# An output projection in 11 matmuls a token tile in place of 12, in a kernel with a planned instruction order

## The chip, the cores and the metric

The kernel runs on one core of a Trainium2 chip. The metric is device time in microseconds (us) of one execution; several executions are timed and the median is given. The engines are TensorE (PE in the profile, its weight loads PEld), VectorE (DVE), ScalarE (ACT), GpSimd (POOL) and SyncE (SP), which here only issues transfers between DRAM and the on-chip memory.

## What is computed

One transformer block on 2048 tokens of 448 features, in float32: layer norm, 16-head attention with 28 features a head and a sliding window of 256 keys, an output projection with a residual, then a second layer norm and a gated feed-forward of width 1792 with a residual.

```python
def _A_ref(x, wqkv, wo):
    B, S, D = x.shape
    H = 16; Dh = D // H; W = 256
    qkv = (x @ wqkv).reshape(B, S, 3, H, Dh).transpose(2, 0, 3, 1, 4)
    q, k, v = qkv[0], qkv[1], qkv[2]
    scores = einsum("bhqd,bhkd->bhqk", q, k) * (Dh ** -0.5)
    mask = (idx[:, None] - idx[None, :] >= 0) & (idx[:, None] - idx[None, :] < W)
    p = softmax(where(mask, scores, -1e9))
    o = einsum("bhqk,bhkd->bhqd", p, v)
    return o.transpose(0, 2, 1, 3).reshape(B, S, D) @ wo

h = x + _A_ref(layernorm(x), wqkv, wo)
y = layernorm(h)
h2 = h + (gelu(y @ w_gate) * (y @ w_up)) @ w_down
```

## The kernel before

**Precision by halves.** Matmuls run on a rounded float32 type (F32R). To keep float32 accuracy, most operands are split into a high half (ACT rounds it, `to_hi`, line 343) and a low half (the remainder, `to_lo`, line 346, on DVE or POOL). A product then takes three matmuls: high x high, high x low, low x high.

**An order made by a planner.** The kernel does not issue instructions as its loops run. Every `op(engine, cost, latency, key, ...)` only enters a list; `Lists.run` then plays the list through a small model of the engines, the 8 PSUM banks, the transfer queue and the port that DVE and POOL share, and emits each engine's instructions in the order in which the model starts them, smallest key first among those that are ready. The constants at the top (LAG_T, LAG_V, EDGE, LN1, LN2, VKEY, MARGIN, LEAD, FETCH and so on) set those keys and some of the model's delays. Each engine runs its list strictly in order on the chip.

**Stages.** Tokens go in four chunks `c` of 512 (four tiles of 128 each). For a chunk: layer norm (`layer_norms`, `normalise`), projections to queries and keys (`project`, seven of them, line 609, each 11 matmuls of 128x512) and to values (`values`, line 564), then four head groups `g` of four heads. A block `B = 4c + g` does scores (657) with a running maximum on DVE (661), the maxima turned and added to the queries (`maxima`, 678 to 692), the scores again the other way round with the exponential on ACT (`probs`, 729 and 733), masks on POOL (`select`, 744), and the product with the values (`attend`, 763).

**Projections go through DRAM.** A projected tile is drained from PSUM into a store buffer (high half by ACT, low half by DVE, lines 612 to 614) and stored by `put` (618, 619) in the form (high, low, high) or its mirror; `loads` (639) brings it back with the features of four heads side by side. The store buffers are given by `pk_at`: a ring of two, and two further ones in `pp` for the projections numbered in PKX.

**Turning normalised tiles.** Features must stand on partitions. `normalise` does it in one of two ways: PE transposes through a PSUM bank (398), then ACT and DVE split it; or, for the tiles in TURNED and for the second layer norm, `turn`: DVE transposes 32x32 blocks (435), four stores to DRAM (439), two loads back (441, 443), then ACT and DVE split it. In the kernel before, tiles 8 to 15 of the first layer norm are turned through DRAM.

**Drain and output.** `drain` (785 to 796) takes a block's result: DVE transposes it (788) into `oblk`, takes the reciprocal of the softmax sums (789), POOL multiplies (786), DVE transposes back (791), ACT and POOL split it into `ohl`. The last block does POOL's part on DVE. In `oblk` each head has 32 places, 28 features and 4 unused ones. After every second block `output` (807) multiplies a pair of groups by the rows of `wo`: for each token tile 2 groups x 3 products of 128x448, so 12 matmuls a tile over both pairs `p`, and DVE adds the result to the residual (810). `wo_weights` (816 to 818) loads and splits the rows of `wo` through one buffer.

**Feed-forward.** From about 341 us PE runs the products of line 945 without a break; a few early ones (969) stand in the last part of attention.

Of the kernel before, what the change touches and what calls it, by code (L numbers as in the profile page):

```python
# [33 lines left out]

LAG_T = 6
LAG_P = 15
LAG_V = 10
EDGE = 8
WIN = 14
FFN = 1000  # L40
LEAD = 90
MARGIN = 0.8
START = 0.8
EARLY = 2
SWAP = -60
HOLDO = 1
AHEAD = 7
BEHIND = 5
LN1 = (0, -20, 70, 134)
LN2 = (166, 231)  # L50
VKEY = (-30, -22, 14, 24)
VHALF = 0
FETCH = 200
POOLED = (3,)
PKX = (2, 3)
PAIRED = 4
TURNED = (8, 9, 10, 11, 12, 13, 14, 15)
# [168 lines left out]
def block_kernel(ctx: ExitStack, tc, x, wqk_in, wv_in, wo_in, ffn_in, out):  # L226
# [10 lines left out]
    def f(ap):  # L237
        return ap.bitcast(F32)
# [12 lines left out]
    one_r = pool.tile([128, 128], F32R, name="one")  # L251
    last_hi = pool.tile([128, 128], F32R, name="lasthi")

    word = pool.tile([128, 88], F32, name="word")
    nhalf = pool.tile([128, 4], F32, name="nhalf")
    e8 = pool.tile([128, 8], F32, name="e8")
    bnst = [pool.tile([128, 6], F32, name=f"bnst{i}") for i in range(2)]
    bnmv = pool.tile([128, 4, 2], F32, name="bnmv")
    bnve = pool.tile([128, 3, 4], F32, name="bnve")
    mx = [pool.tile([128, 2, 4], F32, name=f"mx{i}") for i in range(2)]  # L260
    mhl = [pool.tile([128, 96], F32R, name=f"mhl{i}") for i in range(3)]
    rcp = [pool.tile([128, 16], F32, name=f"rcp{i}") for i in range(2)]
# [54 lines left out]
    def PK(a):  # L317
        return span("proj", 3584 + 512 * a, 512)
# [29 lines left out]
    def dma(key, size, fn, r=(), w=(), cost=0.44, after=()):  # L348
        return op("sp", cost, 0, key, fn, r, w, size=size, after=after)
# [229 lines left out]
           [WQKRAW(m % 2), WQK(m, 0)], [WQK(m, 1)], port=True)  # L579


    pks = [0]

    def pk_at():
        n = pks[0]
        pks[0] += 1
        if n in PKX:
            o = 1792 + 1024 * PKX.index(n)
            return [pp_m[:, o + 512 * i:o + 512 * i + 512].bitcast(F32R) for i in range(2)], \
                pp_m[:, o:o + 1024].rearrange("p (a t) -> p a t", a=2), [span("pp", o // 128 + 4 * i, 4) for i in range(2)]  # L590
        n = sum(k not in PKX for k in range(n)) % 2
        return [pk[:, 2 * n + i] for i in range(2)], f(pk[:, 2 * n:2 * n + 2]), [PK(2 * n + i) for i in range(2)]

    def project(c):
        for m in range(WT):
# [2 lines left out]
    def project_tile(c, m):  # L598
        g, s = divmod(m, 2)
        cc = 12 * (c % 2)  # L600
        hl, both, tok = pk_at()
        B = 4 * c + g
        b = Bank("proj")
        per = 1 if m == 6 else 2
        base = 16 * B - EDGE
        for a in range(NP):
            h, wb, xb = TERMS[a]
            key = -33 + 6 * m + a / 4 if B < 2 else base - WIN * (1 - (s * NP + a) / (per * NP))
            op("pe", mm(512) + 0.002, 0.403, key, lambda a=a, h=h, wb=wb, xb=xb: nc.tensor.matmul(  # L609
                bank[b.k], wqk[m][:, h, wb, :], xT[:, xb, cc * 128:cc * 128 + 512], start=(a == 0),  # L610
                stop=(a == NP - 1)), [span("xT", cc, 4), WQK(m, h)], (), b, tag="proj")
        key = -30 + 6 * m if B < 2 else base
        op("act", 0.49, 0.605, key, lambda: to_hi(hl[0], bank[b.k]), (), [tok[0]], b)
        op("dve", 0.603, 0.698, key, lambda: to_lo(hl[1], bank[b.k], hl[0]), [tok[0]], [tok[1]], b)


        def put(rows, d, name, s, size):
            dma(key, 458 * size, lambda: nc.sync.dma_start(d[:, s:s + 2], both[rows]), tok, [(name, 0)])
            dma(key, 229 * size, lambda: nc.sync.dma_start(d[:, 2 - 2 * s], both[rows, 0]), tok[0:1], [(name, 1)])
        put(slice(0, GF), qk_d[g][c][s], ("d", g, s, c), s, 1)  # L620
        put(slice(GF, 128), qk_d[NG - 1][c][1][16 * m:16 * m + 16], ("d", NG - 1, 1, c, m), 1, 0.15)

# [152 lines left out]
    def drain(B):  # L775
        b, h = acc[B], B % 2
        key = 16 * B + LAG_P + ORDER[5] + LAG_V + 1
        rc = rcp[h]
        ob = oblk.rearrange("p (b r) -> p b r", r=32)


        last = B == NB - 1
        eng, name = (nc.vector, "dve") if last else (nc.gpsimd, "pool")

        def mul():
            eng.tensor_tensor(ob, ob, rc[:, :, None].to_broadcast([128, 16, 32]), op=OP.mult)

        op("dve", 0.63, 0.72, key, lambda: nc.vector.transpose(oblk, bank[b.k]), (), ["oblk"], b)
        op("dve", 0.165, 0.26, key, lambda: nc.vector.reciprocal(rc, ob[:, :, DH]), ["oblk"], [("rcp", h)])
        op(name, 0.6 if last else 1.05, 0.7 if last else 1.06, key + 1, mul, ["oblk", ("rcp", h)], ["oblk"], port=True)  # L790
        op("dve", 0.625, 0.71, key + 2, lambda: nc.vector.transpose(oT, oblk), ["oblk"], ["oT"])
        op("act", 0.52, 0.63, key + 2, lambda: to_hi(ohl[:, h, 0], oT), ["oT"], [("ohl", h, 0)])
        if last:
            exps.append(L.ops[-1])
        op(name, 0.6 if last else 1.25, 0.7 if last else 1.29, key + 3, lambda: to_lo(ohl[:, h, 1], oT, ohl[:, h, 0], eng),
           ["oT", ("ohl", h, 0)], [("ohl", h, 1)], port=True)

    def output(p, c):
        B = 4 * c + 2 * p + 1
        key = 16 * B + LAG_P + ORDER[5] + LAG_V + 5  # L800
        for i in range(4):
            t = c * 4 + i
            k = Bank("task")
            wk = key + (i if B == NB - 1 else 3 * i)
            for a, (h, oh, wh) in enumerate((h, oh, wh) for h in range(2) for oh, wh in ((0, 0), (0, 1), (1, 0))):
                need = [("ohl", h, oh), ("wos", p, h, wh)] if a else [("ohl", h, 0) for h in range(2)] + [("wos", p, h, 0)]
                op("pe", mm(D), 0.38, wk, lambda a=a, h=h, oh=oh, wh=wh, i=i, k=k: nc.tensor.matmul(  # L807
                    bank[k.k][:, 0:D], ohl[:, h, oh, i * 128:(i + 1) * 128], wos[p][:, h, wh], start=(a == 0),
                    stop=(a == 5)), need, (), k, tag="task")
            op("dve", 0.533, 0.626, wk + 1, lambda t=t, k=k: nc.vector.tensor_tensor(  # L810
                hres[:, t, :], bank[k.k][:, 0:D], hres[:, t, :], op=OP.add), [HR(t)], [HR(t)], k)

    def wo_weights(g):
        p, h = divmod(g, 2)
        key = 20 + 16 * p + 5 * h
        dma(key - 20, 224, lambda: nc.sync.dma_start(wo_raw, wo_in[g]), (), [WORAW], after=[got[HOLDO]])
        op("act", 0.47, 0.57, key, lambda: to_hi(wos[p][:, h, 0], wo_raw), [WORAW], [("wos", p, h, 0)])
        op("pool", 1.1, 1.15, key, lambda: to_lo(wos[p][:, h, 1], wo_raw, wos[p][:, h, 0], nc.gpsimd),
           [WORAW, ("wos", p, h, 0)], [("wos", p, h, 1)], port=True)

# [127 lines left out]

    def seen(key, b):

        op("act", 0.08, 0.17, key, lambda: nc.scalar.activation(word[0:1, 0:1], bank[b.k][0:1, 0:1], AF.Copy), (),  # L951
           (), b)

    def product(n, i, c, k, gn, gi, down):
# [224 lines left out]
def layout(inputs):  # L1179

    import numpy as np

    def rows(w):

        w = np.concatenate([w, w[384:]])
        return w.reshape(4, 128, -1).transpose(1, 0, 2)

    wqkv = inputs["A_wqkv"]
    q = [wqkv[:, g * GF:(g + 1) * GF] for g in range(NG)]
    k = [wqkv[:, D + g * GF:D + (g + 1) * GF] for g in range(NG)]  # L1190
    own = [t for g in range(NG - 1) for t in (q[g], k[g])] + [q[NG - 1]]
    wo = np.zeros((NG, 4, 32, D), np.float32)
    wo[:, :, 0:DH] = inputs["A_wo"].reshape(NG, 4, DH, D)
    gate, up = inputs["B_w_gate"], inputs["B_w_up"]
    ffn = [np.concatenate([rows(gate[:, n:n + 128]).reshape(128, 512), rows(up[:, n:n + 128]).reshape(128, 512),
                           inputs["B_w_down"][n:n + 128]], axis=1) for n in range(0, F, 128)]
    return {"x": inputs["A_x"],
            "wqk": np.stack([rows(np.concatenate([t, k[NG - 1][:, 16 * m:16 * m + 16]], axis=1))
                             for m, t in enumerate(own)]),
            "wv": np.stack([rows(wqkv[:, 2 * D + 2 * GF * p:2 * D + 2 * GF * (p + 1)]) for p in range(2)]), "wo": wo.reshape(NG, 128, D), "ffn": np.stack(ffn)}  # L1200


# [19 lines left out]
```

## Time and profile before

| what | us |
|---|---|
| median of three runs | 733.01 (732.46 to 734.0) |
| the profiled execution, whole | 733.24 |
| its span, first to last instruction | 731.5 |

The page of the profile has the busy time of each engine, the span in 40 slices, the transfers, the chain of work that ended last, and groups of instructions by source line. "out<-in" names the tiles that an instruction writes and reads; a line such as L346 is that of a helper, so the tile names tell what it does. "Idle before" is the time for which an engine stood still just ahead of these instructions, with what it waited for. The granted clock of TensorE is full throughout. Matmul ends are modelled, so the time from one start to the next in a run of matmuls is a better price than the mean duration.

### The profile page before, as it was taken

How to read it: one execution, taken by the hardware profiler on the slowest of the kernel's cores; microseconds unless marked ns; L12 is line 12 of the kernel's file. 1: busy time of each engine (PE TensorE's matmuls, PEld its weight loads, DVE VectorE, ACT ScalarE, POOL GpSimd, SP SyncE). 2: the span in 40 equal slices, each digit the busy share in tenths (PEclk: the TensorE clock that was granted, in tenths of full speed). 3: DMA queues.
4: the chain of work that ended last, by engine and by line, in shares of the span. 5: the costliest groups of instructions: out<-in, count | busy, mean ns of one | idle time of the engine just before them, and what ended most of it. 6: DMA issues, size and time to landing. Idle time of an engine off the chain costs nothing.

```text
span 731.5 us, 15121 instructions
## 1 busy us (share of the span) xinstructions
PE 719.3 (98%) x5732; PEld 594.6 (81%) x5732; DVE 404.7 (55%) x1069; ACT 368.0 (50%) x934; POOL 155.7 (21%) x250
## 2 busy tenths in 40 slices
PE   8999999999999999999999999999999999999997
PEld 7886777777778787778888888888888888888886
DVE  7967778978798768858454223144223243233224
ACT  7647667787787678985443222243222233222221
POOL 5505443444344346541000000000000000000000
PEclk9999999999999999999999999999999999999999
DMA  8887787696677868341832000012100000001012
GB/s 307 268 269 234 207 251 184 179 260 200 176 184 196 224 190 239 86 111 26 199 120 84 1 1 3 1 42 84 43 1 1 2 1 1 2 1 51 7 46 101
DMA packets 102801, 83.80 MB, mean 115 GB/s; under 512 B 49272, under 2 KB 92472, under 8 KB 102712
## 3 DMA queue, kind: packets, MB, share of 16 engines
q1 hardware_dynamic: 102584, 82.72, 39.3%
q8 instruction: 45, 0.74, 0.4%
q14 instruction: 28, 0.23, 0.1%
q10 hardware_dynamic: 144, 0.11, 0.0%
HBM read 51.09 MB, written 31.95 MB: 114 GB/s over the span
## 4 chain that ended last, share of the span: by engine, by line
PE 91%; DMA 3%; ACT 3%; DVE 1%; issue 1%; SPq 0%; POOL 0%; DVEq 0%; ACTq 0%; POOLq 0%
PE bank L945 52%; PE bank L609 9%; PE bank L729 6%; PE bank L657 6%; PE bank L807 5%; PE bank L763 5%; PE bank L564 5%; PE bank L969 2%; DMA k<-proj 1%; ACT pp L733 1%; DMA xT<-xn 1%; DMA hres<-in_x_dram 1%; ACT xT L343 1%; ACT rq L343 0%; DMA xn<-xn 0%
## 5 line engine op out<-in xcount | busy, mean ns | idle before, releaser
L661 DVE CUSTOM_DVE_ANT_0 mt<-bank,mt 128x384 bf16<-128x384 f32 (+2 forms) x256 | 127.4, 525 | 33.0 <-PE bank L657 30.7
L733 ACT ACTIVATE pp<-bank 128x384 f32<-128x384 f32 (+2 forms) x352 | 123.0, 387 | 42.8 <-PE bank L729 37.4
L1011 DVE TENSOR_TENSOR mt<-bank,mt 128x512 f32<-128x512 f32 x54 | 37.1, 687 | 142.9 <-ACT mt L1009 142.9
L729 PE MATMUL bank<-rq,rk 104*128 104x384 f32 (+2 forms) x352 | 99.7, 306 | 3.1 <-ACT pp L733 1.7
L744 POOL TENSOR_SCALAR_AFFINE_SELECT pp<-pp 128x512 f32<-128x512 f32 x120 | 75.3, 641 | 110.3 <-ACT pp L733 108.7
L609 PE MATMUL bank<-xT 128*128 128x512 f32 x308 | 96.2, 401 | 0.0
L1009 ACT ACTIVATE mt<-bank 128x512 f32<-128x512 f32 x54 | 32.2, 596 | 118.3 <-PE bank L945 118.3
L729 PEld LDWEIGHTS bank<-rq,rk 104*128 104x128 f32 x352 | 65.3, 189 | 21.2 <-ACT pp L733 9.0
L945 PE MATMUL bank<-xT,rec 64*128 64x512 f32 x656 | 82.0, 388 | 0.0
L945 PE MATMUL bank<-xT,rk 64*128 64x512 f32 x656 | 82.0, 388 | 0.0
L657 PE MATMUL bank<-rk,rq 84*128 84x384 f32 (+2 forms) x256 | 80.3, 342 | 1.0 <-DMA rk<-k 0.8
L945 PEld LDWEIGHTS bank<-xT,rec 64*128 64x128 f32 x656 | 63.0, 184 | 12.2
L945 PEld LDWEIGHTS bank<-xT,rk 64*128 64x128 f32 x656 | 63.0, 184 | 12.2
L1047 DVE TENSOR_TENSOR hres<-bank,hres 128x448 f32<-128x448 f32 (+1 forms) x65 | 35.7, 610 | 66.5 <-PE bank L945 64.7
L945 PE MATMUL bank<-xT,proj 64*128 64x512 f32 x533 | 66.7, 388 | 0.3 <-ACT word L951 0.3
L951 ACT ACTIVATE word<-bank 1x1 f32<-1x1 f32 x162 | 25.6, 158 | 82.2 <-PE bank L945 81.6
L609 PEld LDWEIGHTS bank<-xT 128*128 128x128 f32 x308 | 55.7, 189 | 6.6 <-ACT xT L343 0.2
L945 PEld LDWEIGHTS bank<-xT,proj 64*128 64x128 f32 x533 | 51.1, 184 | 10.5 <-ACT word L951 0.6
L657 PEld LDWEIGHTS bank<-rk,rq 84*128 84x128 f32 x256 | 46.7, 189 | 11.7 <-issue 2.9
L564 PE MATMUL bank<-proj,xT 128*128 128x448 f32 (+1 forms) x220 | 51.1, 336 | 0.0
L343 ACT ACTIVATE rq<-bank 8x512 fp32r<-8x512 f32 x64 | 37.5, 586 | 17.6 <-PE bank L688 16.6
L763 PE MATMUL bank<-pp,v 128*29 128x384 f32 (+2 forms) x704 | 45.4, 388 | 0.0
(138 smaller groups left out, 1086.8 us busy)
## 6 DMA issues: line engine op xcount, KB each, us to landing
rk<-k SPq DMA_DIRECT2D x44, 336.0 KB
rq<-q SPq DMA_DIRECT2D x32, 336.0 KB
q<-proj SPq DMA_DIRECT2D x15, 448.0 KB
v<-in_ffn_dram SPq DMA_DIRECT2D x7, 736.0 KB
k<-proj SPq DMA_DIRECT2D x11, 448.0 KB
xn<-xn SPq DMA_DIRECT2D x88, 56.0 KB
xT<-xn SPq DMA_DIRECT2D x24, 192.0 KB
raw<-in_ffn_dram SPq DMA_DIRECT2D x6, 736.0 KB
```

Of the source, the lines that this page charges most:

```text
L343: nc.scalar.activation(dst, src, AF.Copy)
L564: op("pe", mm(224 * n), 0.29 if n == 1 else 0.38, key + a / 16, lambda a=a, h=h, wb=wb, xb=xb: nc.tensor.matmul(bank[b.k][:, 0:224 * n], x ...
L609: op("pe", mm(512) + 0.002, 0.403, key, lambda a=a, h=h, wb=wb, xb=xb: nc.tensor.matmul(bank[b.k], wqk[m][:, h, wb, :], xT[:, xb, cc * 128 ...
L657: nc.tensor.matmul(bank[b.k][:, o:384], rq[u][0:3 * DH, j, i * 128:i * 128 + 128], rk[u][0:3 * DH, j, m0 * 128:(i + 3) * 128], start=True, ...
L661: nc.vector.tensor_tensor_reduce(junk[s % 2][:, o:384], bank[b.k][:, o:384], mask[:, o:384], 1.0, -BIG, OP.add, OP.max, mx[i // 2][:, i % ...
L729: nc.tensor.matmul(bank[b.k][:, 0:n], rk[u][0:104, j, m * 128:m * 128 + 128], rq[u][0:104, j, lo * 128:(hi + 1) * 128], start=True, stop=True)
L733: nc.scalar.activation(pp[:, j, o * 128:o * 128 + n], bank[b.k][:, 0:n], AF.Exp, scale=SCALE)
L744: nc.gpsimd.affine_select(a, a, pattern=[[0, 4], [-cm, 128]], compare_op=op_, fill=0.0, base=0, channel_multiplier=cm)
L763: nc.tensor.matmul(bank[b.k][32 * j:32 * j + DH + 1, lo * 128:(hi + 1) * 128], v[:, at_v(4 * c - 2 + m), 4 * g + j, :], pp[:, j, at[m] * 1 ...
L807: op("pe", mm(D), 0.38, wk, lambda a=a, h=h, oh=oh, wh=wh, i=i, k=k: nc.tensor.matmul(bank[k.k][:, 0:D], ohl[:, h, oh, i * 128:(i + 1) * 1 ...
L945: nc.tensor.matmul(bank[bk.k][:, 0:n], w, m, start=bool(start), stop=bool(stop), tile_position=(64 * x, 0), skip_group_check=True)
L1011: op("dve", 0.605, 0.702, key + 2 * NP, lambda: nc.vector.tensor_tensor(blocks(g2), src(1), blocks(g2), op=OP.mult), [*G2, *held[1]], G2, ...
```

## The change

The first head group's 28 features a head are kept in another way. Features 0 to 15 stand twice in the 32 places of the head. Features 16 to 27 go into the 4 unused places of the other three groups, four to each group. The rows of `wo` are laid out on the host accordingly, with five blocks in place of four. For the first group one matmul takes the high half with weights that hold the high half in one copy's rows and the low half in the other's, and a second takes the low half with the high weights; the third is gone. `drain` multiplies in several pieces and copies the kept features in. Beside that: tiles 8 to 11 leave TURNED, `put` stores the high halves in both their places with one transfer and the low half with another, a third store buffer in `raw` joins the ring from the seventh projection on, two small tiles are merged into others, and constants of the planner change.

```diff
-LAG_V = 10
-EDGE = 8
+LAG_V = 12
+EDGE = 9
-LEAD = 90
-MARGIN = 0.8
+LEAD = 30
+MARGIN = 0.7
-LN1 = (0, -20, 70, 134)
-LN2 = (166, 231)
-VKEY = (-30, -22, 14, 24)
+LN1 = (0, -19, 55, 134)
+LN2 = (166, 224)
+VKEY = (-30, -23, 14, 24)
-FETCH = 200
+FETCH = 170
+PKS = 3
-TURNED = (8, 9, 10, 11, 12, 13, 14, 15)
+TURNED = (12, 13, 14, 15)
...
+    kept_m = pool.tile([128, 96], F32, name="kept")
+    kept = [m.rearrange("p (b r) -> p b r", r=12) for m in (v_m[:, 8 * VT:8 * VT + 96], kept_m)]
...
         if n in PKX:
-            o = 1792 + 1024 * PKX.index(n)
-            return [pp_m[:, o + 512 * i:o + 512 * i + 512].bitcast(F32R) for i in range(2)], \
-                pp_m[:, o:o + 1024].rearrange("p (a t) -> p a t", a=2), [span("pp", o // 128 + 4 * i, 4) for i in range(2)]
-        n = sum(k not in PKX for k in range(n)) % 2
-        return [pk[:, 2 * n + i] for i in range(2)], f(pk[:, 2 * n:2 * n + 2]), [PK(2 * n + i) for i in range(2)]
+            m, o, name = pp_m, 1792 + 1024 * PKX.index(n), "pp"
+        else:
+            k = ring[0]
+            ring[0] = (k + 1) % (2 if n < WT - 1 else PKS)
+            if k < 2:
+                return [pk[:, 2 * k + i] for i in range(2)], f(pk[:, 2 * k:2 * k + 2]), [PK(2 * k + i) for i in range(2)]
+            m, o, name = raw_m, 0, "raw"
...
         def put(rows, d, name, s, size):
-            dma(key, 458 * size, lambda: nc.sync.dma_start(d[:, s:s + 2], both[rows]), tok, [(name, 0)])
-            dma(key, 229 * size, lambda: nc.sync.dma_start(d[:, 2 - 2 * s], both[rows, 0]), tok[0:1], [(name, 1)])
+            n = rows.stop - rows.start
+            dma(key, 458 * size, lambda: nc.sync.dma_start(
+                d[:, 0:3 - s:2 - s], both[rows, 0:1].to_broadcast([n, 2, 512])), tok[0:1], [(name, 0)])
+            dma(key, 229 * size, lambda: nc.sync.dma_start(d[:, 1 + s], both[rows, 1]), tok[1:2], [(name, 1)])
...
-        def mul():
-            eng.tensor_tensor(ob, ob, rc[:, :, None].to_broadcast([128, 16, 32]), op=OP.mult)
+        def mul(o, lo, n, b=slice(0, 16)):
+            eng.tensor_tensor(o, ob[:, b, lo:lo + n], rc[:, b, None].to_broadcast([128, b.stop - b.start, n]), op=OP.mult)
+        g = B % NG
+        half = [slice(0, 8), slice(8, 16)]
+        steps = [(0.4, lambda i=i: mul(kept[i], 16, 12, half[i]), [], [KEPT[i]]) for i in range(2)] + \
+            [(0.62, lambda o=o: mul(ob[:, :, o:o + 16], 0, 16), [], ["oblk"]) for o in (16, 0)] if not g else \
+            [(0.98, lambda: mul(ob[:, :, 0:DH], 0, DH), [], ["oblk"])] + \
+            [(0.2, lambda i=i: eng.tensor_copy(ob[:, half[i], DH:32], kept[i][:, :, 4 * g - 4:4 * g]), [KEPT[i]],
+              ["oblk"]) for i in range(2)]
...
-        op(name, 0.6 if last else 1.05, 0.7 if last else 1.06, key + 1, mul, ["oblk", ("rcp", h)], ["oblk"], port=True)
+        for cost, fn, rd, wr in steps:
+            cost *= 0.58 if last else 1
+            op(name, cost, cost + 0.05, key + 1, fn, ["oblk", ("rcp", h), *rd], wr, port=True)
...
-            for a, (h, oh, wh) in enumerate((h, oh, wh) for h in range(2) for oh, wh in ((0, 0), (0, 1), (1, 0))):
+            terms = [(h, oh, wh) for h in range(2) for oh, wh in
+                     (((0, 0), (1, 1)) if p == h == 0 else ((0, 0), (0, 1), (1, 0)))]
+            for a, (h, oh, wh) in enumerate(terms):
...
+        if not g:
+
+            a, b = wos[0][:, 0, 0], wos[0][:, 0, 1]
+            for i, d in ((0, b), (1, a)):
+                dma(key - 20, 224, lambda i=i: nc.sync.dma_start(wo_raw, wo_in[i]), (), [WORAW], after=[got[HOLDO]])
+                op("act", 0.47, 0.57, key, lambda d=d: to_hi(d, wo_raw), [WORAW], [("wos", 0, 0, 1 - i)])
+            op("pool", 1.1, 1.15, key, lambda: to_lo(a, wo_raw, a, nc.gpsimd), [WORAW, ("wos", 0, 0, 0)],
+               [("wos", 0, 0, 0)], port=True)
+            op("pool", 1.1, 1.15, key, lambda: nc.gpsimd.tensor_tensor(a, f(a), f(b), op=OP.add),
+               [("wos", 0, 0, 0), ("wos", 0, 0, 1)], [("wos", 0, 0, 0)], port=True)
+            return
...
-    wo = np.zeros((NG, 4, 32, D), np.float32)
-    wo[:, :, 0:DH] = inputs["A_wo"].reshape(NG, 4, DH, D)
+    w = inputs["A_wo"].reshape(NG, 4, DH, D)
+    wo = np.zeros((NG + 1, 4, 32, D), np.float32)
+    for i in range(2):
+        wo[i, :, 16 * i:16 * i + 16] = w[0, :, 0:16]
+    wo[2:, :, 0:DH] = w[1:]
+    for g in range(1, NG):
+        wo[g + 1, :, DH:] = w[0, :, 12 + 4 * g:16 + 4 * g]
```

More of the change, by code (lines that the diff above doesn't have):

```diff
@@ L252, in block_kernel @@
     last_hi = pool.tile([128, 128], F32R, name="lasthi")
-    word = pool.tile([128, 88], F32, name="word")
-    nhalf = pool.tile([128, 4], F32, name="nhalf")
+    kept_m = pool.tile([128, 96], F32, name="kept")
     e8 = pool.tile([128, 8], F32, name="e8")
@@ L258, in block_kernel @@
     bnmv = pool.tile([128, 4, 2], F32, name="bnmv")
-    bnve = pool.tile([128, 3, 4], F32, name="bnve")
+    bnve_m = pool.tile([128, 16], F32, name="bnve")
+    bnve = bnve_m[:, 0:12].rearrange("p (a i) -> p a i", a=3)
+    nhalf = bnve_m[:, 12:16]
     mx = [pool.tile([128, 2, 4], F32, name=f"mx{i}") for i in range(2)]
@@ L309, in block_kernel @@
     WORAW = span("raw", 1024, 448)
+    KEPT = [span("vm", 8 * VT, 96), "kept"]
     def WVRAW(p, b):
@@ L579, in wqk_split @@
            [WQKRAW(m % 2), WQK(m, 0)], [WQK(m, 1)], port=True)
-    pks = [0]
+    pks, ring = [0], [0]
     def pk_at():
@@ L587, in pk_at @@
         if n in PKX:
-            o = 1792 + 1024 * PKX.index(n)
-            return [pp_m[:, o + 512 * i:o + 512 * i + 512].bitcast(F32R) for i in range(2)], \
-                pp_m[:, o:o + 1024].rearrange("p (a t) -> p a t", a=2), [span("pp", o // 128 + 4 * i, 4) for i in range(2)]
-        n = sum(k not in PKX for k in range(n)) % 2
-        return [pk[:, 2 * n + i] for i in range(2)], f(pk[:, 2 * n:2 * n + 2]), [PK(2 * n + i) for i in range(2)]
+            m, o, name = pp_m, 1792 + 1024 * PKX.index(n), "pp"
[5 more added lines that the diff above has]
+            m, o, name = raw_m, 0, "raw"
+        unit = 128 if name == "pp" else 1
+        return [m[:, o + 512 * i:o + 512 * i + 512].bitcast(F32R) for i in range(2)], \
+            m[:, o:o + 1024].rearrange("p (a t) -> p a t", a=2), \
+            [span(name, (o + 512 * i) // unit, 512 // unit) for i in range(2)]
     def project(c):
@@ L808, in output @@
                     bank[k.k][:, 0:D], ohl[:, h, oh, i * 128:(i + 1) * 128], wos[p][:, h, wh], start=(a == 0),
-                    stop=(a == 5)), need, (), k, tag="task")
+                    stop=(a == len(terms) - 1)), need, (), k, tag="task")
             op("dve", 0.533, 0.626, wk + 1, lambda t=t, k=k: nc.vector.tensor_tensor(
@@ L815, in wo_weights @@
         key = 20 + 16 * p + 5 * h
-        dma(key - 20, 224, lambda: nc.sync.dma_start(wo_raw, wo_in[g]), (), [WORAW], after=[got[HOLDO]])
+        if not g:
[8 more added lines that the diff above has]
+            return
+        dma(key - 20, 224, lambda: nc.sync.dma_start(wo_raw, wo_in[g + 1]), (), [WORAW], after=[got[HOLDO]])
         op("act", 0.47, 0.57, key, lambda: to_hi(wos[p][:, h, 0], wo_raw), [WORAW], [("wos", p, h, 0)])
@@ L949, in seen @@
     def seen(key, b):
-        op("act", 0.08, 0.17, key, lambda: nc.scalar.activation(word[0:1, 0:1], bank[b.k][0:1, 0:1], AF.Copy), (),
+        op("act", 0.08, 0.17, key, lambda: nc.scalar.activation(e8[0:1, 0:1], bank[b.k][0:1, 0:1], AF.Copy), (),
            (), b)
@@ L1199, in layout @@
                              for m, t in enumerate(own)]),
-            "wv": np.stack([rows(wqkv[:, 2 * D + 2 * GF * p:2 * D + 2 * GF * (p + 1)]) for p in range(2)]), "wo": wo.reshape(NG, 128, D), "ffn": np.stack(ffn)}
+            "wv": np.stack([rows(wqkv[:, 2 * D + 2 * GF * p:2 * D + 2 * GF * (p + 1)]) for p in range(2)]), "wo": wo.reshape(NG + 1, 128, D), "ffn": np.stack(ffn)}
 def kernel(**inputs):
```

## The prediction

> **What bounds the kernel now.** I read the page's head first, then the busy time by stage, then what TensorE waits for, then the chain of work that ended last.
>
> ```profile
> span 731.5 us, 15121 instructions
> ...
> PE 719.3 (98%) x5732; PEld 594.6 (81%) x5732; DVE 404.7 (55%) x1069; ACT 368.0 (50%) x934; POOL 155.7 (21%) x250
> ```
>
> PE (TensorE) is busy for 719.3 of 731.5 us; no other engine passes 55%. The average hides two stages, so the next view cuts the span: columns are the stretch, its length, busy us (and count) of PE, of its weight loads, of VectorE (DVE), ScalarE (ACT) and GpSimd (POOL), then granted clock, DMA share and GB/s.
>
> ```profile
> 0.00:40.00 40.00, 37.19 (x223) 32.53 (x224) 33.31 (x73) 28.36 (x49) 21.63 (x54) 1.00 0.89 290
> 40.00:80.00 40.00, 38.86 (x235) 29.52 (x234) 28.80 (x117) 24.41 (x57) 12.53 (x17) 1.00 0.82 244
> 80.00:120.00 40.00, 38.11 (x240) 30.64 (x238) 32.36 (x112) 29.12 (x71) 17.48 (x25) 1.00 0.78 222
> 120.00:200.00 80.00, 79.19 (x554) 61.37 (x554) 65.17 (x211) 61.92 (x158) 35.26 (x52) 1.00 0.72 197
> 200.00:280.00 80.00, 79.15 (x555) 64.36 (x552) 63.02 (x212) 60.04 (x153) 38.76 (x59) 1.00 0.73 196
> 280.00:341.00 61.00, 60.25 (x416) 45.52 (x414) 46.43 (x124) 51.22 (x131) 26.98 (x38) 1.00 0.46 117
> 341.00:731.50 390.50, 386.54 (x3520) 330.63 (x3519) 135.66 (x226) 112.91 (x318) 3.06 (x8) 1.00 0.12 38
> ```
>
> The reader is to see two things. Attention (0 to 341 us) keeps PE, DVE and ACT all between 70% and 97% busy with the DMA engines at 0.72 to 0.89 for most of it: PE leads by little. The feed-forward (341 to 731.5) is PE and nothing else, and no part of the change shortens a matmul of it. So what is to be won lies before 341, where PE sits idle 2.81 + 1.14 + 1.89 + 0.81 + 0.85 + 0.75 = 8.25 us. The first 40 us (2.81) are the start, which the change hardly touches; 40 to 120 us has 3.03, the rest 2.41: together 5.44.
>
> The longest idle pieces have names (us in total, times, longest):
>
> ```profile
> PE bank L729 <- ACT pp L733: 1.7, 4, 0.9
> PE bank L688 <- DVE mhl L681: 1.2, 1, 1.2
> PE bank L729 <- ACT rq L343: 1.0, 3, 0.5
> ```
>
> and the chain, in order of time (start, us, what), shows where they come from:
>
> ```profile
> 66.49 3.69 DMA k<-proj
> ...
> 70.20 0.62 ACT proj L343
> ...
> 74.23 4.47 DMA k<-proj
> ...
> 79.80 1.14 DVE xT L346
> ...
> 81.84 0.28 PE bank L688
> ```
>
> Between 66 and 79 us the chain runs twice through a store of projected keys: the drain of a projection waits until an older store has left its buffer, DVE falls behind, and the maxima matmul (L688) is late by the 1.2 us above.
>
> **The change part by part.** *One pass of twelve.* The first head group's three products become two. Per token tile one 128x448 matmul of L807 goes, 16 in all.
>
> ```profile
> 10.84 1.09 PE bank L398 x8
> ...
> 334.66 4.86 PE bank L807 x24
> ```
>
> ```profile
> L807 PE MATMUL bank<-wos,ohl x96: 360/366/472, 87.3 to 316.0; 128*128 128x448 f32 x96
> ```
>
> 24 of them back to back took 4.86 us, so one is 0.2025 us and 16 are **3.24 us**. All sit between 87 and 316 us, in outputs of the first pair (its weights are the tile wos); the serial run at 334.66 belongs to the second pair and keeps its 24. PE is the engine nearest its limit there, so I count it whole: minus 3.24. The lower bound is zero, if PE waits for DVE or ACT instead.
>
> The Trainium skill (Perfetto Trace Analysis, Identifying the Most-Contended Engine) says that matmul busy share overstates how near TensorE is to its limit, and that the busy share of weight loads is the better gauge. Rows above: weight loads are busy 264 of 341 us (77%) before 341 and 331 of 390.5 (85%) behind it, so the trace agrees that attention has slack on PE. By that gauge the pass would be worth 3.24 x 77 / 85 = 2.9 us.
>
> *Tiles 8 to 11 go back to TensorE.* TURNED loses 8 to 11, so L398 gains 16 transposes. Eight took 1.09 us in the chain, 0.136 each: **plus 2.18**. Bounds: zero, if they fall into the 3.03 us of idle time, and 16 x 0.292 = 4.7, if none overlaps its neighbour.
>
> ```profile
> L398 PE MATMUL bank<-ident,xn 128*128 128x128 f32 x32 | 5.2, 292 | 0.7 <-ACT xn L393 0.7
> ```
>
> ```profile
> L435 DVE STREAM_TRANSPOSE xn<-xn 128x448 f32<-128x448 f32 x22 | 13.9, 633 | 1.5 <-DMA xn<-xn 1.3 <-ACT xn L393 0.2
> ...
> L346 DVE TENSOR_TENSOR xT<-xT 128x384 fp32r<-128x384 f32 x24 | 14.7, 611 | 6.6 <-ACT xT L343 6.6
> ...
> L346 DVE TENSOR_TENSOR xT<-xT,lasthi 64x128 fp32r<-64x128 f32 x24 | 9.8, 407 | 0.9
> ...
> L346 DVE TENSOR_TENSOR xT<-bank,xT 128x384 fp32r<-128x384 f32 x8 | 4.4, 554 | 0.1
> ...
> L346 DVE TENSOR_TENSOR xT<-bank,xT 64x128 fp32r<-64x128 f32 x8 | 2.3, 293 | 0.1
> ```
>
> ```profile
> L343 ACT ACTIVATE xT<-xT 128x384 fp32r<-128x384 f32 x24 | 12.5, 519 | 0.1
> ...
> L343 ACT ACTIVATE xT<-xT 64x128 fp32r<-64x128 f32 x24 | 7.4, 309 | 0.4
> ...
> L343 ACT ACTIVATE lasthi<-xT 64x128 fp32r<-64x128 f32 x24 | 7.4, 308 | 0.6
> ...
> L343 ACT ACTIVATE xT<-bank 128x512 fp32r<-128x512 f32 x8 | 4.6, 587 | 0.3 <-PE bank L398 0.3
> ```
>
> ```profile
> L439 SPq DMA_DIRECT2D xn<-xn x88: 308/479/2203, 45.2 to 353.7; - x88
> ```
>
> A tile turned through DRAM costs DVE 0.633 + 0.611 + 0.407 = 1.65 us, a transposed one 0.554 + 0.293 = 0.85; ACT 0.519 + 0.309 + 0.308 = 1.14 against 0.59. Four tiles: DVE minus 3.2, ACT minus 2.2, and 16 small stores and 8 loads leave the SP queue (16 x 0.479 = 7.7 us of issue for the stores alone). None of it is PE time by itself; it shortens what PE waits for. A transposed tile holds one of the two PSUM banks (6, 7) that projections, values and outputs share, for about 0.6 + 0.6 + 0.85 us.
>
> *Third store buffer, stores split by need.*
>
> ```profile
> L346 DVE TENSOR_TENSOR proj<-bank,proj 128x512 fp32r<-128x512 f32 x26 | 17.9, 688 | 10.2 <-ACT proj L343 10.0
> ```
>
> From the seventh projection on, the ring has three buffers, and the large store carries the high halves alone, so it leaves before DVE's low half, 0.69 us earlier. Bytes and number of stores stay. The small store of the low halves is now the one that waits for DVE; the loads `rq<-q` and `rk<-k` queued behind it on SP wait as they did behind the large one. This aims at the 3.69 and 4.47 us pieces. With the four tiles' transfers gone, and the re-laid order (LAG_V, EDGE, LN1, LN2, VKEY, MARGIN), I take back 2.0 of the 3.03 us that PE idles from 40 to 120: **minus 2.0**. This is the least certain term: a whole new order can win all 5.44 us or lose as much again, so its ends are minus 5.4 and plus 5.4; I take the value nearest to the rows that have a named cause there.
>
> *Drain and weights.*
>
> ```profile
> L786 POOL TENSOR_TENSOR oblk<-oblk,rcp 128x512 f32<-128x512 f32 x15 | 15.8, 1050 | 25.6 <-DVE rcp L789 21.3 <-DVE mhl L678 4.0
> ...
> L371 POOL TENSOR_TENSOR bnve<-bnmv,bnve 128x2 f32<-128x2 f32 x15 | 3.3, 218 | 1.2
> ...
> L346 POOL TENSOR_TENSOR wos<-raw,wos 128x448 fp32r<-128x448 f32 x2 | 2.3, 1154 | 1.2 <-ACT wos L343 1.2
> ```
>
> ```profile
> L681 DVE SCALAR_TENSOR_TENSOR mhl<-mx,mhl x32: 122/168/996, 44.3 to 312.6; 128x8 fp32r<-128x8 f32 x32
> ```
>
> 512 elements take 1.05 us on POOL and two take 0.218, so (1.05 - 0.218) / 510 = 1.63 ns an element above some 0.215. First group: two of 96 (0.37) and two of 256 (0.63) elements make 2.0 instead of 1.05; the others one of 448 (0.95) and two copies of 32 (0.27) make 1.49. POOL gains 4 x 0.95 + 11 x 0.44 = 8.6 us on 152 busy in 341, so it has room. Only the second group's 0.44 stands ahead of an output of the first pair, and PE has no listed wait for ohl: nothing. The last drain runs on DVE beside 21 early feed-forward matmuls that end at 334.66, just as its result arrives, so two small copies there may show: **plus 0.2** (bounds 0 and 0.54, two copies at POOL's 0.27). The fifth weight load and its extra POOL sum (1.15) run before 87 us, when the first output starts: nothing.
>
> *FETCH, LEAD:* loads and norms of the feed-forward, covered by PE's unbroken run behind 341: nothing.
>
> **Sum:** -3.24 + 2.18 - 2.0 + 0.2 = -2.9 us. The profiled execution took 733.24 (1.74 around its span), the median 733.01; from the median that is **730.1 us**.
>
> **Rivals.**
> - *The saving is swallowed:* PE's freed slots become waits for DVE and ACT, which are 70% to 85% busy; the pass and the transposes then cancel within 1.1 us and no wait goes. For it: DVE 65 of 80 us from 120 on. Against it: PE is still ahead of them. Time: 733.0 - 3.24 + 2.18 = 731.9, up to 733.9 if the pass is hidden half and the idle time stays.
> - *GpSimd holds DVE up (slower).* In order of time (start, us, engine):
>
> ```profile
> 69.52 1.30 POOL L346 TENSOR_TENSOR ohl<-oT,ohl 128x512 fp32r<-128x512 f32 x1
> 69.85 1.00 DVE L681 SCALAR_TENSOR_TENSOR mhl<-mx,mhl 128x8 fp32r<-128x8 f32 x1
> ...
> 79.43 1.34 POOL L346 TENSOR_TENSOR proj<-raw,proj 128x448 fp32r<-128x448 f32 x1 [0.98 <-ACT proj L343]
> 79.80 1.12 DVE L346 TENSOR_TENSOR xT<-xT,lasthi 64x128 fp32r<-64x128 f32 x1
> ```
>
>   L681 took 1.00 us against a median of 0.168, and the small subtraction 1.12 against 0.293 for the same size from a bank, each until a long POOL operation ended. The second one preceded the 1.2 us wait of L688. The longer drains put more such operations beside the maxima of each block (32 in all). One more such wait costs PE 1.2 us; three of them eat the gain, and from four on it is slower by over 0.2%. Five give 733.0 - 2.9 + 6 = 736.1. Against it: in the trace one of 32 reached PE. The Trainium skill (SBUF — State Buffer, SBUF: two separate sides) has it that VectorE with two SBUF inputs and a GpSimd instruction reading SBUF take one shared port pair in turn, for a whole instruction; the two outliers agree.
> - *The new order wins more:* all 5.44 us of idle time go and the transposes cost nothing: 733.0 - 3.24 - 5.4 = 724.4; half of the idle time with the transposes at half gives 727.9.
> - *The pass does not go:* the matmuls could stay at 12 a tile; the loop builds two terms for p = h = 0, so I give it nothing.
>
> **How the numbers follow.** Forecast (728.5 to 731.5): 0.45. Wins more (726 to 728.5, little below): 0.15. Swallowed (731.5 to 734.5): 0.22. Slower through GpSimd or a worse order (735 to 737): 0.18. The range goes from 726.5 to 735.5: it takes in the swallowed case and the near half of the slower one. A measurement of this kernel tells about 0.2% (1.5 us) from no change; faster by more 0.60, within 0.22, slower 0.18.
>
> **What would show it.** L807 with 176 matmuls; L398 with 48; 72 stores xn<-xn in place of 88; PE idle in 40 to 120 down from 3.03 to about 1; no piece of 3 us or more of `k<-proj` in the chain near 66 to 79. Wrong: L688 or L729 waits grow, L681's mean rises over its 0.27, or PE idles before 341 as long as now.

## The result, and the profile after

| | before, us | changed, us | ratio, 95% interval |
|---|---|---|---|
| median of six runs each | 733.46 (732.46 to 735.19) | 727.84 (727.26 to 728.25) | 0.9921 (0.9907 to 0.9934) |
| profiled execution, whole | 733.24 | 727.88 | |
| its span | 731.5 | 726.2 | |

The change makes the kernel 0.8% faster, 5.6 us by the medians. 2.9 were forecast, so it won almost twice as much.

The head of the page of the changed kernel, to be laid beside the one shown ahead:

```profile
span 726.2 us, 15085 instructions
...
PE 717.8 (99%) x5732; PEld 594.4 (82%) x5732; DVE 401.4 (55%) x1067; ACT 366.4 (50%) x927; POOL 162.6 (22%) x285
```

PE has as many matmuls as before (16 products fewer, 16 transposes more). Its busy time falls by 1.5 us; the time in which it is not busy shrinks more, from 12.2 us to 8.4. The view by stage (stretch, length, then busy us of PE, weight loads, DVE, ACT and POOL, clock, DMA share, GB/s) says where:

```profile
0.00:40.00 40.00, 37.57 (x224) 32.71 (x225) 32.61 (x72) 28.35 (x49) 21.32 (x54) 1.00 0.89 289
40.00:80.00 40.00, 39.66 (x241) 31.85 (x240) 29.70 (x118) 27.41 (x60) 13.43 (x22) 1.00 0.83 251
80.00:120.00 40.00, 39.88 (x260) 31.68 (x259) 33.25 (x117) 30.27 (x76) 19.06 (x29) 1.00 0.68 191
120.00:200.00 80.00, 79.80 (x568) 63.45 (x567) 65.54 (x214) 62.20 (x160) 36.22 (x61) 1.00 0.76 209
200.00:280.00 80.00, 79.53 (x559) 62.26 (x559) 64.02 (x214) 61.66 (x162) 37.33 (x63) 1.00 0.74 203
280.00:341.00 61.00, 59.98 (x417) 46.09 (x418) 44.84 (x122) 45.49 (x115) 34.82 (x55) 1.00 0.34 88
```

From 40 to 120 us PE's idle time falls from 3.03 to 0.34 + 0.12 = 0.46 us, and the matmuls done there rise from 475 to 501. Over the whole 341 us it falls from 8.25 to 4.58. What PE waits for shows the same; of the three waits quoted ahead, of 1.0 to 1.7 us in all, at most 0.5 is left of each, and the one of L729 for ACT rq is no longer listed (L703 and L744 are the lines that were 688 and 729):

```profile
PE bank L1208 <- POOL ident L496: 2.1, 1, 2.1
PE bank L703 <- DVE mhl L696: 0.5, 1, 0.5
PE bank L672 <- DVE mx L676: 0.5, 1, 0.5
PE bank L404 <- ACT xn L399: 0.3, 1, 0.3
PE bank L744 <- ACT pp L748: 0.2, 1, 0.2
```

In the chain (start, us, what) of the stretch where two stores stood before, there is PE alone now:

```profile
60.59 0.44 PE bank L404 x4
...
65.04 0.44 PE bank L404 x4
...
66.81 0.74 PE bank L622 x3
67.55 0.78 PE bank L778 x16
```

The two fours of L404 are transposes that the change brought back from DRAM to TensorE: 0.11 us each, around the place (64 to 66 us) where PE waited for ACT before.

From 80 to 120 us the two longest gaps of PE in the kernel before stand behind the splitting of a turned tile. One is the wait of L688 quoted ahead, behind a DVE subtraction of such a tile (79.80, 1.14 us). The other is 0.94 us long, until 120.30 us, where the exponential of the scores (ACT pp) came after three ACT pieces of such a tile. This is the chain of before:

```profile
118.80 0.42 ACT xT L343
...
119.24 0.31 ACT lasthi L343
...
119.57 0.31 ACT xT L343
119.87 0.38 ACT pp L733
```

In the changed kernel tiles 8 to 11 have no such pieces, and PE has no gap over 0.15 us from 80 to 120.

The unbroken run of the feed-forward began at 341.14 us in the chain of before; in that of the changed kernel (with its last output ahead of it):

```profile
329.85 4.86 PE bank L835 x24
...
336.10 14.00 PE bank L984 x127
```

So 5.0 of the span's 5.3 us are won ahead of the feed-forward.

### The profile page after: what moved, and what is told of

Same layout as the page of the kernel before. It is cut to its first block, busy times and chain, and to the rows that moved or that the text cites. A ratio compares the mean times of both kernels' runs of the same rounds, so it can differ in the third digit from the quotient of the medians.

```text
span 726.2 us, 15085 instructions
## 1 busy us (share of the span) xinstructions
PE 717.8 (99%) x5732; PEld 594.4 (82%) x5732; DVE 401.4 (55%) x1067; ACT 366.4 (50%) x927; POOL 162.6 (22%) x285
## 4 chain that ended last, share of the span: by engine, by line
PE 94%; DVE 2%; ACT 1%; issue 1%; DMA 1%; POOL 0%; SPq 0%; DVEq 0%; POOLq 0%
PE bank L984 53%; PE bank L622 10%; PE bank L744 6%; PE bank L672 6%; PE bank L778 5%; PE bank L570 5%; PE bank L835 5%; PE bank L1008 3%; DMA hres<-in_x_dram 1%; PE bank L404 1%; DVE mt L676 1%; PE bank L703 0%; ACT pp L748 0%; DVE hres L1086 0%; ACT xT L349 0%
## 5 line engine op out<-in xcount | busy, mean ns | idle before, releaser
L744 PE MATMUL bank<-rq,rk 104*128 104x384 f32 (+2 forms) x352 | 97.6, 303 | 0.6 <-ACT pp L748 0.2
L744 PEld LDWEIGHTS bank<-rq,rk 104*128 104x128 f32 x352 | 65.0, 189 | 17.4 <-ACT pp L748 5.9
L984 PEld LDWEIGHTS bank<-xT,rk 64*128 64x128 f32 x656 | 63.0, 184 | 12.2
L984 PEld LDWEIGHTS bank<-xT,rec 64*128 64x128 f32 x656 | 63.0, 184 | 12.1
L990 ACT ACTIVATE e<-bank 1x1 f32<-1x1 f32 x162 | 25.7, 158 | 81.2 <-PE bank L984 80.5
L672 PEld LDWEIGHTS bank<-rk,rq 84*128 84x128 f32 x256 | 46.3, 189 | 12.2 <-DVE mx L676 5.2
```

The lines of the kernel that those rows point to most:

```text
L672: nc.tensor.matmul(bank[b.k][:, o:384], rq[u][0:3 * DH, j, i * 128:i * 128 + 128], rk[u][0:3 * DH, j, m0 * 128:(i + 3) * 128], start=True, ...
L744: nc.tensor.matmul(bank[b.k][:, 0:n], rk[u][0:104, j, m * 128:m * 128 + 128], rq[u][0:104, j, lo * 128:(hi + 1) * 128], start=True, stop=True)
L984: nc.tensor.matmul(bank[bk.k][:, 0:n], w, m, start=bool(start), stop=bool(stop), tile_position=(64 * x, 0), skip_group_check=True)
```

## The experiments

Ratios are to the kernel before, run beside each on the same chip. Most of these kernels lay a new order, since the planner lays all instructions anew when one number changes. Two keep an order exactly (b_pass, a_pass), and b_fill adds to that of TensorE alone.

**One pass less, the order kept (b_pass).**

```diff
-lambda a=a, ...: nc.tensor.matmul(bank[k.k][:, 0:D], ohl[...], wos[p][:, h, wh], ...)
+lambda a=a, ...: (p, a) == (0, 1) or nc.tensor.matmul(bank[k.k][:, 0:D], ohl[...], wos[p][:, h, wh], ...)
```

> The kernel before, its order of instructions unchanged, without the 16 products high x low of the first group in the output projection (they are planned and not issued, so the result lacks that product). Theory 1, PE sets the pace in attention: 16 x 0.2025 = 3.2 us faster, 733.5 to about 730.3. Theory 2, the freed slots become waits for DVE and ACT: under 1 us.

732.71 us, ratio 0.9984 (0.9973 to 0.9995): 1.2 us faster (0.4 to 2.0 by the interval), not 3.2. At equal clock it is less: the five runs at a mean clock of 0.999 or 1.000 have a median of 732.05, and those of before beside them 732.65. In this fixed order at least a third, and by the middle value nearly two thirds, of the freed PE time is not won. The profile does not show it as waits either: PE's busy time falls by 1.2 us (719.3 to 718.1), and its idle time stays at 12.1. The matmuls around the freed places take the rest up; what holds them is not shown.

**The pass back, in the changed kernel's order (a_pass).**

```diff
-lambda a=a, ...: nc.tensor.matmul(...)
+lambda a=a, ...: [nc.tensor.matmul(...) for _ in range(2 if (p, a) == (0, 1) else 1)]
```

> The changed kernel, its order of instructions unchanged, with the second product of the first group's output (low half times the high weights) issued twice in a row for each of the 16 tiles, so 12 products a tile again; the result then has that product doubled. Theory 1, PE is the bound and the pass is worth its full price in the new order: 16 x 0.2025 = 3.2 us slower, 731.1. Theory 2, as in b_pass (1.2 us of 3.2): 729 to 729.5, the rest falls into waits.

730.36 us, ratio 0.9949 (0.9935 to 0.9963) against 0.9921 for the change: 0.28% or 2.1 us for 16 matmuls. The medians alone differ by 2.5 us, all at a clock of 0.999 or 1.000. The two intervals together leave about 0.6 to 3.5 us, so the full price of 3.24 is not excluded here. That a matmul is worth more in the order with less idle time fits the two middle values, but the intervals overlap and do not show it. In the profiles, PE's busy time rises by 1.4 us (717.8 to 719.2), as it fell in b_pass; another 1.4 is idle time in the first 40 us (2.43 to 3.81), ahead of any output.

**Each other part alone, added to the kernel before (b_turn, b_buf, b_const).**

```diff
-TURNED = (8, 9, 10, 11, 12, 13, 14, 15)
+TURNED = (12, 13, 14, 15)
```

> The kernel before with tiles 8 to 11 taken out of TURNED and nothing else; the planner lays a new order. Theory 1 (the fewer transfers and the DVE and ACT time of these tiles are what takes PE's idle time of 40 to 120 us away): plus 2.2 of transposes, minus 2 to 2.6 of idle time, so 733 to 734 and idle time in 40 to 120 us near 0.5. Theory 2 (transposes cost and the idle time is due to stores and keys): about 735.5, idle time as before near 3.

731.70 us, ratio 0.9962 (0.9949 to 0.9974): 2.8 us faster, better than either theory; the one run at a clock of 1.000 took 730.71, 1.9 us less than the 732.65 of before at such a clock. Both numbers hold a new order too. From 40 to 120 us PE idles 0.70 us in place of 3.03 (windows of b_turn):

```profile
40.00:80.00 40.00, 39.30 (x237) 29.66 (x239) 30.01 (x122) 26.00 (x59) 13.29 (x20) 1.00 0.83 252
80.00:120.00 40.00, 40.00 (x265) 32.87 (x258) 33.79 (x122) 31.07 (x74) 19.19 (x25) 1.00 0.73 191
```

For b_buf, the diff of `pk_at` and `put` as in the change and nothing else:

> The kernel before with the third store buffer and the stores split by need, nothing else. If the waits for store buffers made the idle time of 40 to 120 us: 2 to 2.6 us faster, about 731, and idle time there near 0.5. If not: within 1 us of before, idle time near 3.

738.76 us, ratio 1.0059 (1.0046 to 1.0072): 4.3 us slower, as neither theory had it. From 40 to 120 us PE idles 1.04 us in place of 3.03, so the idle time went the way of the first theory and the time did not. Its profile names one cause. Windows of 4 us (columns as above):

```profile
96.00:100.00 4.00, 4.00 (x38) 3.06 (x34) 2.47 (x8) 2.65 (x8) 2.37 (x5) 1.00 0.64 163
100.00:104.00 4.00, 3.58 (x13) 2.08 (x13) 3.52 (x12) 3.87 (x10) 1.54 (x2) 1.00 1.09 255
104.00:108.00 4.00, 3.86 (x13) 2.48 (x17) 3.52 (x12) 3.08 (x8) 2.68 (x5) 0.52 0.79 248
108.00:112.00 4.00, 4.00 (x24) 1.85 (x17) 2.27 (x7) 0.65 (x2) 1.47 (x2) 0.62 0.90 189
112.00:116.00 4.00, 4.00 (x30) 3.47 (x32) 3.10 (x14) 3.30 (x11) 0.64 (x1) 1.00 0.20 42
116.00:120.00 4.00, 3.93 (x35) 3.16 (x28) 3.45 (x11) 2.86 (x9) 0.64 (x1) 1.00 0.78 209
120.00:124.00 4.00, 3.58 (x13) 1.91 (x12) 3.56 (x14) 3.95 (x9) 1.82 (x3) 1.00 0.64 143
124.00:128.00 4.00, 4.00 (x20) 3.21 (x23) 3.04 (x12) 2.97 (x8) 2.31 (x3) 0.58 0.02 4
```

Look at the matmuls beside the busy share: from 100 to 104 us PE has 13 of them, 12 with 384 columns. By the 0.2025 us of 448 columns, such a one is worth some 0.17 us (an estimate), so this is 2.1 us of work in 4, though PE is called busy for 3.58. (Counts compare only roughly: many of the neighbour's 38 are short.) Right behind, the granted clock halves: 0.52 and 0.62 in two windows make 4 x (0.48 + 0.38) / 0.5 = 6.9 us at half clock. At 120 us the same again, 13 matmuls and then 0.58, 3.4 us at half.

Some 10 us at half clock can cost up to 5 us of PE's time. They are a part of the loss and not all of it: three runs of this kernel at a mean clock of 0.995 have a median of 738.38, and the two of before at 0.995 took 735.42 and 736.21, so about 2.6 us of loss stand at equal clock. Its own parts are thus neither shown to help nor to harm the time.

The Trainium skill (TensorE: Matmul & The Clock Gate, Part 1: The HAM clock gate) has a clock that falls to one half after an idle window of about 3.4 us, on windows that run free of the program. The 6.9 and 3.4 us agree with that length; "idle" does not hold as it stands, since PE still ran 13 matmuls in such a stretch.

For b_const, the planner's eight constants of the change and nothing else:

> The kernel before with the planner's new constants (LAG_V, EDGE, LEAD, MARGIN, LN1, LN2, VKEY, FETCH) and nothing else. If the order by itself takes the waits away: 2 to 3.5 us faster, 730 to 731.5. If the constants only suit the other parts of the change: within 1.5 us of before, or slower.

734.75 us, ratio 1.0001 (0.9991 to 1.0011): no difference, as in the second case of the expectation.

**Each part undone in the changed kernel (a_turn, a_buf, a_const).** The three edits above, the other way.

> The changed kernel with tiles 8 to 11 turned through DRAM again, a new order laid by the planner. By b_turn (2.8 us gained alone): 730.5 to 731, with idle PE time between 40 and 120 us back at 2 to 3 us. If the order matters more than this part: within 1 us of 727.8 or past 732.

736.44 us, ratio 1.0025 (1.0012 to 1.0039): against 0.9921, 7.6 us lost, past 732 as expected if the order matters more. The idle time is back as well, 2.70 us from 40 to 120:

```profile
40.00:80.00 40.00, 39.76 (x234) 31.80 (x232) 27.26 (x114) 25.87 (x59) 12.08 (x19) 1.00 0.86 243
80.00:120.00 40.00, 37.54 (x232) 27.38 (x231) 32.50 (x110) 29.44 (x70) 20.80 (x33) 0.96 0.80 215
```

Its longest gap there, 0.97 us, again ends with an exponential that came after the three ACT pieces of a turned tile (103.69 to 104.77 us in its chain). The mean clock is 0.96 from 80 to 120 us and 0.94 from 280 to 341.

> The changed kernel with a ring of two store buffers and the stores of before. By b_buf (4.3 us lost alone): 724 to 726, faster than the change. If b_buf's loss was its order's two stretches of half clock (104 and 125 us) and not the part itself: 727 to 730, no clock below 1 before 341 us.

733.51 us, ratio 0.9987 (0.9974 to 0.9999): 4.8 us lost, outside both cases of the expectation; single runs between 730.99 (mean clock 1.000) and 735.61 (0.992). The four at 0.999 or 1.000 have a median of 731.8, still 4.0 us above the changed kernel.

> The changed kernel with the planner's constants of before. By b_const (nothing gained alone): within 1 us of 727.8. If the constants were what fits the order to the other parts: 729.5 to 733, with PE idle between 40 and 341 us above the 2.2 us of the changed kernel, or a stretch of half clock.

733.94 us, ratio 0.9996 (0.9985 to 1.0006): 5.5 us lost. Its runs at a clock of 0.999 or 1.000 stand at 732.5 to 732.7, so most of that is waits and not the clock. By its edit this is a run of the next kind too: it changes no operation, only the order.

Alone, the four parts give -1.2 - 2.8 + 4.3 + 0.0 = +0.3 us; taken away one by one they cost 2.1 + 7.6 + 4.8 + 5.5 = 20 us. Neither adds up to 5.6, and the pieces of the drain, the fifth block of weights and the merged tiles were not run by themselves. Something other than the parts is in each of these numbers.

**Another order of the same work (a_n1, a_n3, b_n3).** No operation is changed here, only a number by which the planner chooses.

```diff
-MARGIN = 0.7
+MARGIN = 0.72
```

> The changed kernel with MARGIN 0.72 in place of 0.70, which is no operation's cost on the chip but makes the planner lay another order. If the gain lies in the parts of the change: within 1 us of the changed kernel, a ratio to before of 0.991 to 0.994. If a good part lies in this one order: 1.5 to 6 us slower than it, like the three undone parts, a ratio of 0.994 to 1.000.

734.55 us, ratio 1.0009 (0.9994 to 1.0025): 6.4 us slower than the changed kernel. In its profile, PE idles 2.57 us from 200 to 280, where the changed kernel has 0.47, and its clock is 0.98 there and 0.97 after:

```profile
200.00:280.00 80.00, 77.43 (x521) 59.46 (x524) 63.42 (x201) 61.28 (x161) 40.63 (x66) 0.98 0.77 206
280.00:341.00 61.00, 59.50 (x399) 43.26 (x391) 43.22 (x128) 44.99 (x112) 28.97 (x48) 0.97 0.30 74
```

```diff
-EASE = {"py": 0.0, "pe": 0.05, ...}
+EASE = {"py": 0.0, "pe": 0.06, ...}
```

> The changed kernel with the planner's tolerance for TensorE (EASE) 0.06 in place of 0.05: again only another order. Same numbers as for the first such run: 0.991 to 0.994 if the parts make the gain, 0.994 to 1.000 if the order does.

731.03 us, ratio 0.9966 (0.9950 to 0.9982): 3.3 us slower than the changed kernel.

The clock is not what makes these two slower: their runs at 0.999 or 1.000 have medians of 733.20 (five of a_n1) and 730.77 (four of a_n3), 5.4 and 2.9 us above the changed kernel's 727.84 at such a clock.

The same edit to the kernel before:

> The kernel before with the same tolerance 0.06 in place of 0.05: another order of the same work. If the order is what varies: 1.5 to 6 us away from before. If not: within 1 us.

737.54 us, ratio 1.0051 (1.0035 to 1.0068): 3.7 us slower than before. Here most of it is the clock: none of its runs is above 0.995, and against the two runs of before at 0.995 (735.42 and 735.62) its three at that clock (median 736.72) are 1.2 us slower. In the order, with the clock that it brings, there are thus 3 to 6 us, as much as in the whole change.

One thing does go with the parts and not with the order: where PE idles. From 80 to 120 us it idles 0.80 to 2.54 us in the six profiles in which tiles 8 to 11 go through DRAM (before, b_pass, b_buf, b_const, b_n3, a_turn), and 0.00 to 0.58 in the seven in which they do not. From 40 to 80 us it idles 0.24 to 0.35 us in six profiles with the new buffers and stores and 0.70 to 1.67 in the six without; a_const, with them and at 1.04, is the one exception. (b_fill, whose idle time was filled, is left out.) From 120 to 341 us the order decides: 1.69 us in the changed kernel, 4.35, 3.02 and 3.83 in a_n1, a_n3 and a_const, which do the same work.

**Idle TensorE time filled (b_fill).** If thin stretches cost clock, work that nobody needs should make the kernel before faster.

```diff
-WARM = 26.0
+WARM = 340.0
```

> The kernel before with idle TensorE time that the planner foresees up to 340 us (not only up to 26 us) filled by 60 further transposes that nobody reads; the orders of the other engines stay. If idle PE time lets the granted clock fall to half for stretches of about 3.4 us, and the slower runs of before (734 to 736 at a mean clock of 0.995 to 0.998, against 732.5 at 1.000) are those: more runs at clock 0.999 and above, median 0.5 to 1.5 us lower than before's. If the clock has nothing to do with idle time: the same spread, and up to 60 x 0.109 = 6.5 us slower where the transposes delay other work.

732.56 us, ratio 0.9983 (0.9973 to 0.9993): 60 transposes more and 1.4 us less. All 12 runs have a mean clock of 0.999 or 1.000; of the 24 runs of before beside them, 9 have. Those 24 by clock:

| mean granted clock | runs | median us |
|---|---|---|
| 0.999 and above | 9 | 732.87 |
| 0.997 and 0.998 | 12 | 734.39 |
| 0.995 and below | 3 | 735.62 |

So the median of before holds about 1.0 us of half clock here (733.92 against 732.87). One place where it can come from shows in the chain of b_fill, and in the windows of b_n3:

```profile
64.11 0.90 PE bank L1169 x8
65.01 0.17 PE bank L657 x2
65.18 0.23 PE bank L729
65.41 0.22 PE bank L1169 x2
```

```profile
62.27:66.27 4.00, 3.04 (x27) 1.72 (x25) 2.32 (x11) 2.16 (x5) 1.51 (x2) 1.00 0.76 198
66.27:69.69 3.42, 3.38 (x10) 2.94 (x11) 2.24 (x10) 2.52 (x6) 1.04 (x2) 0.50 1.07 264
...
120.00:124.00 4.00, 2.87 (x13) 1.66 (x13) 2.90 (x9) 3.77 (x10) 2.15 (x3) 1.00 0.72 151
124.00:128.00 4.00, 4.00 (x40) 3.10 (x40) 2.04 (x8) 2.62 (x6) 1.52 (x3) 1.00 0.83 204
```

The kernel before idles at the same place, and in its profiled execution the clock stayed full there and behind it:

```profile
62.90:66.90 4.00, 3.00 (x27) 1.64 (x25) 2.35 (x10) 2.53 (x5) 1.10 (x2) 1.00 0.80 231
```

b_fill puts ten transposes into 64 to 66 us. In b_n3 PE is busy for 3.04 of 4 us up to 66.27, and the clock is at one half from there to 69.69. A thin stretch is no certain sign, though: from 120 to 124 us b_n3 has 13 matmuls and 2.87 us of busy time, and the clock stays at 1.00. In the changed kernel the eight transposes quoted from its chain stand around this place; all six of its runs had a clock of 0.999 or 1.000.

## Why the prediction was right, and what was off

The sign was right and the measured time lies in the stated range. That says little for the sum: the range was 9 us wide, and 727.84 lies below the forecast band of 728.5 to 731.5, in the band of the rival "the new order wins more", which had a chance of 0.15. (Its "half of the idle time with the transposes at half" comes to 728.1 when added up again, not 727.9; "swallowed" with the pass hidden half to 733.6, not 733.9.) The signs named for the mechanism all came: 176 products of the output, 48 transposes, 72 stores, idle time of 0.46 us from 40 to 120, and no store of keys in the chain near 66 to 79. So the mechanism, less idle time of PE ahead of the feed-forward, is the one that the profile shows, but the sum had its largest term elsewhere, in the pass, and was near by errors that partly cancel. The sizes, step by step:

- *One pass of twelve, minus 3.24, "I count it whole".* Oversized by the middle values. With the order held, 16 matmuls are worth 1.2 us in the old one and 2.1 in the new, so 95 to 99% busy did not mean that PE alone sets the pace. The 2.9 by the share of the weight loads is too high for the old order as well. The rival "the saving is swallowed" was right in size for the larger part of this term, in the order of before, though no new waits are seen. (That PE, DVE and ACT are "all between 70% and 97% busy" does not hold stretch by stretch: from 40 to 80 us ACT has 24.41 of 40 us, 61%, and from 120 us on PE has 99%.)
- *Tiles 8 to 11 back on TensorE, plus 2.18.* As a price of the transposes it is a little high: they run at 0.11 us each, 1.76 in all, against 0.136. Whether they cost even that is not shown. With a new order, the part alone won 2.8 us. What the text called time that "shortens what PE waits for" was then counted in the next term.
- *Idle time, minus 2.0 of the 3.03 from 40 to 120 us.* Too small: 2.57 there, and 3.67 in all before 341 us. The text named the stores of keys as its cause, beside the tiles and the order. The buffers go with the idle time from 40 to 80 us (1.14 to 0.34); the larger piece, from 80 to 120 us (1.89 to 0.12), goes with the tiles, in each order that was run; that the transfers or the DVE and ACT pieces of the tiles make it was not tested apart, but both long gaps there stand behind such pieces. For the time, no gain of the third buffer and the split stores alone was shown.
- *Drain, plus 0.2; weights, nothing.* No run has it by itself. The 24 products of the last output took 4.86 us in both chains and follow the matmuls ahead of them without a gap, so nothing of the 0.2 is seen. POOL gained 6.9 us of busy time against the 8.6 worked out. The pieces came out close to the estimates of 0.95, 0.63, 0.37 and 0.27 us:

```profile
L803 POOL TENSOR_TENSOR oblk<-oblk,rcp 128x448 f32<-128x448 f32 x11 | 10.5, 959 | 9.7 <-DVE rcp L813 9.7
...
L803 POOL TENSOR_TENSOR oblk<-oblk,rcp 128x256 f32<-128x256 f32 x8 | 5.0, 619 | 0.2
...
L809 POOL COPY oblk<-v 128x32 f32<-128x32 f32 x11 | 2.7, 245 | 0.0
...
L803 POOL TENSOR_TENSOR v<-oblk,rcp 128x96 f32<-128x96 f32 x4 | 1.4, 349 | 3.3 <-DVE rcp L813 3.0 <-DVE bnmv L383 0.3
```

- *GpSimd holds DVE up.* The sign named for it came, weakly: the mean of the DVE step ahead of the maxima matmul (L681, now L696) rose from 0.272 to 0.296 us, its longest from 1.00 to 1.28. It did not reach PE: the wait of the maxima matmul for DVE went from 1.2 to 0.5 us, once each.
- *A whole new order, plus or minus 5.4.* Named, and borne out: only another order of the changed kernel lost up to 6.4 us.
- *Missing altogether:* the granted clock. The profile of before showed 1.00 in every slice, since that execution had no stretch at half clock; its other runs did. Of the 5.6 us by the medians, some 0.5 to 0.8 are this, as an estimate: its runs at a clock of 0.999 and above have medians of 732.65 to 732.99 in the three sets of runs made beside the experiments.

The books of the two profiles nearly close: -3.24 for the pass, 16 x 0.11 = +1.76 for the transposes and -3.67 of idle time make -5.15, against -5.3 measured. But this is an account and not a cause, and it puts the pass at a price that b_pass and a_pass do not confirm. Of the 3.67, 2.57 lie from 40 to 120 us, where they go with the two parts in nearly every order; 0.72 lie behind 120 us, where orders of the same work differ by up to 2.7; the rest is in the first 40 us.

**What stays open** is how much of 5.6 us belongs to the parts. With a_const and b_const, which are other orders too, the changed kernel in four orders has ratios of 0.9921, 0.9966, 0.9996 and 1.0009, and before in three has 1, 1.0001 and 1.0051. The means differ by 0.4%, but seven orders that scatter by as much do not settle it. The order that came with the change is the best of its four; the measured gain includes the choice of that order.

## What to carry to other kernels

Where a planner lays the order, an edit changes two things, the work and the order; time a few neutral variations of the order (a tolerance, a margin) before an edit is credited with a few tenths of a per cent, and hold the order fixed to price a single operation. A matmul taken out of a fixed order, or put back into one, was worth a third to two thirds of its price here by the middle values, and 60 transposes put where PE idled cost nothing. Compare the idle time of a stretch over several orders: what stays with an edit in all of them is the edit's. Look at the matmuls and the granted clock in windows of a few us, and at the clock of several executions: here a stretch that is called 90% busy had the clock halve behind it, and one full-clock profile hid what other executions of the same kernel lost.

## What the runs showed of the hardware that was not expected

The granted clock halved behind stretches in which TensorE was thinly used but far from idle: 13 matmuls in 4 us (b_buf from 100 and from 120 us), or 27 short and long ones with 3.04 us of busy time (b_n3 up to 66.27). Such a stretch does not always do it: b_n3 had 13 matmuls and 2.87 us from 120 to 124 us, and the clock stayed full. Neither the count nor the busy share parts the two kinds here; what does stays open. It halved in some runs of a kernel and not in others (15 of 24 runs of before had a mean of 0.998 or less). Transposes that nobody reads kept it up: 12 of 12 runs at 0.999 or above. A mean clock of 0.9975 is 734 x 0.0025 / 0.5 = 3.7 us at half, about one such stretch, and it costs about 1.5 us of the run: 734.39 against 732.87.
